# Moving the output weights' sums, the buffers of three pairs and the places of the output splits in a fused retention and feed-forward kernel

## The chip, the cores and the metric

The kernel runs on one core of one Trainium2 chip. The metric is the device time of one execution in microseconds (us): the median of 3 timed runs is 597.18, from 596.79 to 597.63. A separate execution was recorded by the profiler.

## The reference

Three stages follow one another. Stage 1 is a retention layer (batch 2, 8 heads, 768 positions, head size 64) worked in blocks of 64; its output, 1536 tokens by 512, is the input of two feed-forward layers, all in float32:

```
x  = retention(q, k, v, lam)                 # 1536 x 512
h  = x @ w_in;  x1 = relu(h)**2 @ w_out      # 512 -> 2048 -> 512
y  = sigmoid(x1 @ w_gate) * (x1 @ w_val)     # 512 -> 1536
out = y @ w_out2                             # 1536 -> 512
```

## The kernel before, in words

**Precision.** TensorE (PE) multiplies in a rounded float32 format. Each operand is therefore kept as a high part, a rounded copy made by ScalarE (ACT), and a low part, value minus high part, made by VectorE (DVE). Each product takes three matmuls: high by high, high by low, low by high. "Copy" below is the making of a high part, "split" the making of a low part; a tile cannot be used until both are done.

**Tiles.** Tokens lie in three blocks of 512 (TB). The first block goes through a layer directly (`step_1`, `step_2`: `stage_a` multiplies by the input weights, `elem` applies the nonlinearity, `stage_b` multiplies by the output weights); the other two blocks are worked together as a 2 x 2 block product by Strassen's scheme with seven products instead of eight (`strassen`). In the last layer this gives four stretches that the change touches:

- the gate and value stage, 12 steps of 36 matmuls (`step_2`), each with three weight tiles whose low parts `wlo` are made by `split_w` for the next step; in its first half the remaining weights are still converted (`conv_act`, `conv_dve`) and stored in DRAM;
- the pair stage, `strassen` with twelve keys `(2, i, u)`: pairs i = 0 to 5 of hidden tiles, u = 0 for the gate, u = 1 for the value. A key has seven blocks of six matmuls (`block`, L678). ACT takes copies `s` of accumulators (`snap`), DVE adds them (`total`, L692); `use_gate` applies the sigmoid, `use_val` multiplies (L796). Accumulators are added to twice, so a later block of a key waits for the copy or addition that reads the earlier contents;
- the output stage, `blocks_out`: two halves q = 0 and 1 of the output columns, each again with seven products (`PRODUCTS`), each product a sum over the six pairs in groups (`ORDER`); each group is 21 matmuls (42 for the last, with two pairs). For pair i it needs seven matrices, made by sums and differences of the hidden blocks (`raw[0]` to `raw[6]`, made in `use_val` and `later`), as copies and splits in `gq[i]`, and seven combinations of the output weights in `wq[q, i]`;
- the sums of the output weights, `sum_out_w(i)`: a load of two weight tiles (`wr`), four subtractions on DVE (`ws`, L914) and four stores to DRAM; `prepare_w(q, n, i, load, pos)` later loads them into one of two fixed places (`D` and `rows`, taken in turn), copies (L938) and splits (L942) them.

**Seven matrices of a pair.** For pair 0 they go from the raw tiles straight to `gq` (`direct`), with 2.0 us of plan time between pieces. For pairs 4 and 5 `direct` is used too, 0.8 apart, at the places in `DIRECT`. Pairs 1 to 3 (`VIA_DRAM`) are stored as they are made and come back by `through_dram`: three loads of 512 KB and one of 256 KB, with copies (L883) and splits (L886) 1024 or 512 columns wide. Pairs 1 and 2 give up their buffers after q = 0 and are loaded a second time for q = 1.

**Order.** The program is a fixed list. `clock` adds up the time of the matmuls issued (0.2267 us each), and `at(pos, fn)` puts a piece of work on an agenda that is flushed after each block: everything due by the plan's clock is then issued, sorted by place. Every engine takes its instructions in that order and runs ahead as far as its inputs and buffers allow. T4 is the plan's time at which the pair stage starts, T5 that of the output stage, T6 = T5 + 28.56 that of its second half. Loads and most stores are issued by SyncE (SP), also in order.

**Buffers.** `up` has 27 buffers of 2 KB per partition (`unit`), `wp` 27 of 4 KB (`double`), PSUM 8 banks. A tile takes a free buffer when its first instruction is issued, and waits for the readers of the tile that had it before.

Of the kernel before, what the change touches and what calls it, by code (L numbers as in the profile page):

```python
# [38 lines left out]
def retention_moe_kernel(  # L39
# [747 lines left out]
    def pair_in_2(i):  # L787
        gate = {}

        def use_gate(di, t, c, in_psum):  # L790
            r = gate[di, t] = unit("r")
            nc.scalar.activation(r, c, AF.Sigmoid)

        def use_val(di, t, c, in_psum):
            g = unit("g")
            nc.vector.tensor_tensor(out=g, in0=c, in1=gate.pop((di, t)), op=ALU.mult)  # L796
            n = GB.get((di, t))
            raw[n] = g
            if n is not None:
                done(n)  # L800
            if n == 5:
                later()

        raw = {}

        def done(n):
            if i in VIA_DRAM:
                g = raw[n]
                at(clock[0] + 2.5, lambda: nc.sync.dma_start(out=gs_dram[i, :, n], in_=g))

        def total(n, a, b, op):
            raw[n] = unit("gs")
            nc.vector.tensor_tensor(out=raw[n], in0=raw[a], in1=raw[b], op=op)
            done(n)

        def later():


            t = clock[0]
            at(t + 1.5, lambda: total(0, None, 6, ALU.add))  # L820
            at(t + 3.5, lambda: total(1, 0, 4, ALU.subtract))
            at(t + 5.5, lambda: total(2, 4, None, ALU.subtract))
            at(t + 7.5, lambda: total(3, 5, 1, ALU.subtract))
            at(t + 7.5, lambda: direct(i, raw) if i not in VIA_DRAM else raw.clear())

        return [use_gate, use_val]

    GB = {(0, 0): 4, (1, 0): 5, (1, 1): 6}
    VIA_DRAM = (1, 2, 3)
    PIECES = ((0, 1), (2, 3), (4, 5), (6,))  # L830
    gq, wq = {}, {}

# [13 lines left out]
    def block_of(pieces, n):  # L846
        return pieces[n // 2][:, n % 2]

    def direct(i, raw):

        pos = clock[0] if i == 0 else DIRECT[i]
        raw = dict(raw)

        def hi(n):
            if i not in gq:
                new_set(i)
            nc.scalar.copy(block_of(gq[i][0], n), raw[n])

        def lo(n):
            nc.vector.tensor_tensor(  # L860
                out=block_of(gq[i][1], n), in0=raw.pop(n), in1=block_of(gq[i][0], n),
                op=ALU.subtract,
            )

        gap = 2.0 if i == 0 else 0.8
        for k, n in enumerate((4, 5, 1, 0, 2, 3, 6)):
            at(pos + gap * k, lambda n=n: hi(n))
            at(pos + gap * k + 1.2, lambda n=n: lo(n))

    DIRECT = {}  # L870

    def through_dram(i, load, pos):
        raw = {}
# [273 lines left out]
    with tc.manual_schedule():  # L1147
# [97 lines left out]
        for k in range(3 * NF2 - n_out):  # L1245
            convert(T3 + 2.0 + 3.6 * k)
        for i in range(NF2 // 2):
            sum_out_w(i, T4 - 24.0 + 8.0 * i)
        keys = [(2, i, u) for i in range(NF2 // 2) for u in range(2)]
        prepare_a(keys[0], T4)  # L1250
        at(T4 - 28.0, lambda: combine_a((2, 0, 1)))
# [2 lines left out]
        for f in range(NF2):  # L1254
            step_2(f)
        T6 = T5 + 6 * STEP
        through_dram(1, T5 - 13.0, T5 - 6.5)
        through_dram(2, T5 - 4.5, T5 + 0.5)
        through_dram(3, T5 + 1.0, T5 + 6.0)
        DIRECT.update({4: T5 + 11.0, 5: T5 + 16.5})  # L1260
        for n, i in enumerate((0, 1, 2, 3, 4, 5)):
            prepare_w(0, n, i, T5 - 13.5 + STEP * n, T5 - 6.0 + STEP * n)
        for n, i in enumerate((5, 4, 3, 0, 2, 1)):
            prepare_w(1, n, i, T6 - 13.5 + STEP * n, T6 - 6.0 + STEP * n - (2.0 if n == 5 else 0))
        through_dram(2, T6 - 1.0, T6 + 4.8)
        through_dram(1, T6 + 4.0, T6 + 10.0)
        uses = [use for i in range(NF2 // 2) for use in pair_in_2(i)]
        strassen(keys, uses, (None, lambda: close(2)))
        blocks_out()
# [64 lines left out]
```

## Time and profile before

| | before |
|---|---|
| median of 3 timed runs | 597.18 us |
| profiled execution: time | 597.77 us |
| profiled execution: span, first to last instruction | 596.0 us |
| PE busy | 575.7 us (97%) |
| DVE busy | 472.0 us (79%) |
| ACT busy | 366.7 us (62%) |
| granted TensorE clock over the span | 0.999 of full speed |
| pair stage, from its first matmul | 406.34 us |
| output stage, from its first matmul | 533.09 us |

Times in the rows below are microseconds from the span's start. In a row of a timeline the first number is the start, the second the duration from the first to the end of the last of its merged instructions; then the engine, the line of the program, the operation, the tiles (written <- read), the shapes, and "x3" for three instructions. In brackets stands how long the engine was idle before it and whose result ended the wait. Ends of matmuls are modelled, so the distance between starts is the better measure on PE.

### The profile page before, as it was taken

The numbers are of one execution on the slowest core, as the hardware profiler recorded it, in microseconds if no ns is written. First come the engines' busy times: TensorE is split into PE (matmuls) and PEld (weight loads), VectorE is DVE, ScalarE is ACT, GpSimd is POOL, SyncE is SP. The second block draws the span as 40 slices with busy tenths as digits, with TensorE's granted clock in tenths as the row PEclk, the third lists the DMA queues.
The fourth block names the chain that finished last, engine by engine and source line by source line (L and its number), as shares of the span: only waits on it lengthen the run. The fifth ranks groups of instructions, "written<-read, shape, count | busy, mean of one in ns | idle before, by whom it ended". The sixth has DMA issues, their size and how long they took to land.

```text
span 596.0 us, 8997 instructions
## 1 busy us (share of the span) xinstructions
PE 575.7 (97%) x3172; PEld 470.6 (79%) x3172; DVE 472.0 (79%) x726; ACT 366.7 (62%) x599; POOL 47.2 (8%) x48
## 2 busy tenths in 40 slices
PE   8899999989999999999999999999799999989996
PEld 8788888767888888888888888888578888868875
DVE  2689896899788868988777887775789777779964
ACT  4579999996565647666556655534455456377450
POOL 1751100000000000000000000201022210000000
PEclk9999999999999999999999999999999999999999
DMA  8999886772263397999978756857878767445581
GB/s 255 413 405 388 301 291 212 258 286 73 73 210 112 124 328 278 415 410 412 406 244 293 246 174 206 247 175 263 265 183 213 197 196 223 155 158 212 182 321 72
DMA packets 66128, 147.16 MB, mean 247 GB/s; under 512 B 6817, under 2 KB 13985, under 8 KB 66082
## 3 DMA queue, kind: packets, MB, share of 16 engines
q1 hardware_dynamic: 61776, 140.67, 66.7%
q0 software_dynamic: 3360, 3.93, 4.5%
q10 hardware_dynamic: 946, 1.97, 1.0%
q8 instruction: 25, 0.41, 0.3%
q14 instruction: 21, 0.17, 0.1%
HBM read 104.60 MB, written 40.38 MB: 243 GB/s over the span
## 4 chain that ended last, share of the span: by engine, by line
PE 73%; DVE 10%; DMA 8%; ACT 4%; issue 3%; SPq 1%; POOL 0%; DVEq 0%; ACTq 0%
PE p L678 27%; PE p L1056 15%; PE p L472 12%; PE p L985 8%; PE p L486 7%; DMA a<-w 3%; PE p L315 2%; PE p L400 2%; DMA gr<-gs 1%; DMA wt<-wr 1%; DVE xcl L564 1%; DMA decay<-w_dram 1%; DVE at L350 1%; DVE ws L914 1%; PE p L383 1%
## 5 line engine op out<-in xcount | busy, mean ns | idle before, releaser
L678 PE MATMUL p<-xch,ah 128*128 128x512 f32 x280 | 110.4, 394 | 6.9 <-DVE c L692 5.2
L678 PE MATMUL p<-xch,al 128*128 128x512 f32 x280 | 109.1, 390 | 0.0
L678 PE MATMUL p<-xcl,ah 128*128 128x512 f32 x280 | 109.1, 390 | 0.0
L678 PEld LDWEIGHTS p<-xch,ah 128*128 128x128 f32 x280 | 52.6, 188 | 22.2 <-DVE c L692 6.5
L678 PEld LDWEIGHTS p<-xch,al 128*128 128x128 f32 x280 | 52.6, 188 | 11.1
L678 PEld LDWEIGHTS p<-xcl,ah 128*128 128x128 f32 x280 | 52.6, 188 | 10.5
L687 ACT COPY s<-p 128x512 f32<-128x512 f32 x60 | 35.1, 587 | 40.2 <-PE p L678 40.0
L985 PE MATMUL p<-gq,wq 128*128 128x512 f32 x252 | 58.1, 391 | 1.1 <-DVE wq L942 1.1
L985 PEld LDWEIGHTS p<-gq,wq 128*128 128x128 f32 x252 | 47.1, 188 | 11.9 <-DVE wq L942 2.3
L155 ACT ACTIVATE j<-raw 128x512 f32<-128x512 f32 x68 | 45.7, 672 | 13.9 <-issue 5.3
L460 DVE TENSOR_TENSOR wlo<-u,whi 128x512 fp32r<-128x512 f32 x68 | 46.1, 708 | 10.1 <-ACT whi L458 8.1
L692 DVE TENSOR_TENSOR c<-p,s 128x512 f32<-128x512 f32 x60 | 41.1, 686 | 15.5 <-PE p L678 15.1
L181 DVE CUSTOM_DVE_ANT_0 u<-m,r 128x1024 uint16<-128x1024 uint16 x68 | 48.7, 717 | 4.8 <-ACT r L161 1.7
L1056 PE MATMUL p<-g2h,whi 128*128 128x512 f32 x128 | 49.8, 389 | 0.0
L1056 PE MATMUL p<-g2l,whi 128*128 128x512 f32 x128 | 49.8, 389 | 0.0
L1056 PE MATMUL p<-g2h,wlo 128*128 128x512 f32 x128 | 49.8, 389 | 0.0
L472 PE MATMUL p<-xh,wlo 128*128 128x512 f32 x160 | 43.5, 394 | 3.3 <-DVE wlo L460 3.3
L472 PE MATMUL p<-xh,whi 128*128 128x512 f32 x160 | 43.2, 392 | 0.0
L472 PE MATMUL p<-xl,whi 128*128 128x512 f32 x160 | 42.8, 390 | 0.0
L163 ACT ACTIVATE r<-raw 128x512 int32<-128x512 uint32 x52 | 34.6, 666 | 6.9 <-PE p L1056 3.7
L472 PEld LDWEIGHTS p<-xh,wlo 128*128 128x128 f32 x160 | 29.6, 188 | 11.5 <-DVE wlo L460 5.6
L458 ACT CAST whi<-u 128x512 fp32r<-128x512 f32 x68 | 37.9, 615 | 0.5 <-PE p L472 0.5
(127 smaller groups left out, 1043.2 us busy)
## 6 DMA issues: line engine op xcount, KB each, us to landing
raw<-in_w SPq DMA_DIRECT2D x68, 512.0 KB, 6.5
w<-u SPq DMA_DIRECT2D x68, 256.0 KB, 4.6
u<-w SPq DMA_DIRECT2D x52, 256.0 KB, 4.6
a<-w SPq DMA_DIRECT2D x20, 512.0 KB, 4.1
g<-g SPq DMA_DIRECT2D x32, 256.0 KB, 4.4
g<-g SPq DMA_DIRECT2D x16, 512.0 KB, 7.8
gr<-gs SPq DMA_DIRECT2D x15, 512.0 KB, 5.5
kv<-in_kv SPq DMA_DIRECT2D x11, 512.0 KB, 10.1
```

The source lines that it names most:

```text
L155: nc.scalar.activation(j, t[:, :, 1].bitcast(F32), AF.Copy, scale=2.0**-112)
L163: nc.scalar.activation(r, low, AF.Copy, scale=2.0**-29)
L181: nc.vector.tensor_tensor(out=w.bitcast(I32), in0=m, in1=r, op=ALU.add)
L458: nc.scalar.copy(hi, src)
L460: lambda lo=lo, src=src, hi=hi: nc.vector.tensor_tensor(out=lo, in0=src, in1=hi, op=ALU.subtract)
L472: nc.tensor.matmul(acc, lhsT=a[:, kk * P : (kk + 1) * P], rhs=b[:, kk, :], start=i == 0, stop=i == 11,)
L486: nc.tensor.matmul(acc[e], lhsT=a[:, e * P : (e + 1) * P], rhs=b, start=first and i == 0, stop=last and i == 2,)
L678: nc.tensor.matmul(acc, lhsT=w[:, col, kk * P : (kk + 1) * P], rhs=x[:, kk, :], start=start and i == 0, stop=stop and i == 5, skip_group_c ...
L687: nc.scalar.copy(s, acc)
L692: nc.vector.tensor_tensor(out=c, in0=acc, in1=s, op=ALU.add)
L985: nc.tensor.matmul(acc[k], lhsT=a[:, wn], rhs=block_of(b, gn), start=first and n == 0, stop=last and n == 3 * len(group) - 1,)
L1056: nc.tensor.matmul(acc[e, t], lhsT=a[:, e * P : (e + 1) * P], rhs=b[:, t, :], start=first and i == 0, stop=last and i == 2,)
```

## The change

- In the pair stage `later` makes pair 5's four totals 7.5 us of plan time later. Its call at the end now has three cases: pairs in `VIA_DRAM` drop their raw tiles; pair 0 is copied and split by `by_unit` with 4.5 us between pieces; pair 5 by `by_unit` at T5 + 16.5, 0.8 apart.
- `VIA_DRAM` takes in pair 4, so its seven matrices are stored and come back by `through_dram`.
- `by_unit_through_dram` is new: seven loads of 256 KB into 2 KB buffers, 0.7 apart, then `by_unit`. It is used for pair 1 in the first half and for pairs 2 and 1 in the second; before, these used `through_dram` and 4 KB buffers.
- `sum_out_w(i)` is due at T4 - 64 + 9i instead of T4 - 24 + 8i (its load 9 before, its stores 4 after).
- The loads and copies of `prepare_w` stand at places listed one by one instead of at a regular distance.

```diff
@@ -816,17 +816,22 @@
         def later():
 
 
-            t = clock[0]
+            t = clock[0] + (7.5 if i == 5 else 0.0)
             at(t + 1.5, lambda: total(0, None, 6, ALU.add))
             at(t + 3.5, lambda: total(1, 0, 4, ALU.subtract))
             at(t + 5.5, lambda: total(2, 4, None, ALU.subtract))
             at(t + 7.5, lambda: total(3, 5, 1, ALU.subtract))
-            at(t + 7.5, lambda: direct(i, raw) if i not in VIA_DRAM else raw.clear())
+            if i in VIA_DRAM:
+                at(t + 7.5, raw.clear)
+            elif i == 0:
+                at(t + 7.5, lambda: by_unit(i, dict(raw), clock[0], 4.5))
+            else:
+                at(t + 7.5, lambda: by_unit(i, dict(raw), T5 + 16.5, 0.8))
 
         return [use_gate, use_val]
 
     GB = {(0, 0): 4, (1, 0): 5, (1, 1): 6}
-    VIA_DRAM = (1, 2, 3)
+    VIA_DRAM = (1, 2, 3, 4)
     PIECES = ((0, 1), (2, 3), (4, 5), (6,))
     gq, wq = {}, {}
 
@@ -846,10 +851,7 @@
     def block_of(pieces, n):
         return pieces[n // 2][:, n % 2]
 
-    def direct(i, raw):
-
-        pos = clock[0] if i == 0 else DIRECT[i]
-        raw = dict(raw)
+    def by_unit(i, raw, pos, gap):
 
         def hi(n):
             if i not in gq:
@@ -862,12 +864,20 @@
                 op=ALU.subtract,
             )
 
-        gap = 2.0 if i == 0 else 0.8
         for k, n in enumerate((4, 5, 1, 0, 2, 3, 6)):
             at(pos + gap * k, lambda n=n: hi(n))
             at(pos + gap * k + 1.2, lambda n=n: lo(n))
 
-    DIRECT = {}
+    def by_unit_through_dram(i, load, pos):
+        raw = {}
+
+        def bring(n):
+            raw[n] = unit("gr")
+            nc.sync.dma_start(out=raw[n], in_=gs_dram[i, :, n])
+
+        for k, n in enumerate((4, 5, 1, 0, 2, 3, 6)):
+            at(load + 0.7 * k, lambda n=n: bring(n))
+        by_unit(i, raw, pos, 0.8)
 
     def through_dram(i, load, pos):
         raw = {}
@@ -1245,7 +1255,7 @@
         for k in range(3 * NF2 - n_out):
             convert(T3 + 2.0 + 3.6 * k)
         for i in range(NF2 // 2):
-            sum_out_w(i, T4 - 24.0 + 8.0 * i)
+            sum_out_w(i, T4 - 64.0 + 9.0 * i)
         keys = [(2, i, u) for i in range(NF2 // 2) for u in range(2)]
         prepare_a(keys[0], T4)
         at(T4 - 28.0, lambda: combine_a((2, 0, 1)))
@@ -1254,16 +1264,22 @@
         for f in range(NF2):
             step_2(f)
         T6 = T5 + 6 * STEP
-        through_dram(1, T5 - 13.0, T5 - 6.5)
-        through_dram(2, T5 - 4.5, T5 + 0.5)
-        through_dram(3, T5 + 1.0, T5 + 6.0)
-        DIRECT.update({4: T5 + 11.0, 5: T5 + 16.5})
-        for n, i in enumerate((0, 1, 2, 3, 4, 5)):
-            prepare_w(0, n, i, T5 - 13.5 + STEP * n, T5 - 6.0 + STEP * n)
-        for n, i in enumerate((5, 4, 3, 0, 2, 1)):
-            prepare_w(1, n, i, T6 - 13.5 + STEP * n, T6 - 6.0 + STEP * n - (2.0 if n == 5 else 0))
-        through_dram(2, T6 - 1.0, T6 + 4.8)
-        through_dram(1, T6 + 4.0, T6 + 10.0)
+        by_unit_through_dram(1, T5 - 14.0, T5 - 7.0)
+        through_dram(2, T5 - 4.0, T5 + 1.5)
+        through_dram(3, T5 + 1.0, T5 + 6.5)
+        through_dram(4, T5 + 6.0, T5 + 11.5)
+        for n, load, pos in (
+            (0, -21.0, -13.0), (1, -12.0, -1.5), (2, -6.0, 4.0),
+            (3, 1.0, 8.8), (4, 6.0, 13.5), (5, 11.0, 18.3),
+        ):
+            prepare_w(0, n, n, T5 + load, T5 + pos)
+        for n, i, load, pos in (
+            (0, 5, -12.5, -5.0), (1, 4, -7.5, -1.0), (2, 3, -3.0, 3.5),
+            (3, 0, 1.0, 8.0), (4, 2, 6.0, 12.5), (5, 1, 10.0, 15.5),
+        ):
+            prepare_w(1, n, i, T6 + load, T6 + pos)
+        by_unit_through_dram(2, T6 - 7.0, T6 + 5.0)
+        by_unit_through_dram(1, T6, T6 + 10.2)
         uses = [use for i in range(NF2 // 2) for use in pair_in_2(i)]
         strassen(keys, uses, (None, lambda: close(2)))
         blocks_out()
```

## Rows read from the trace of the kernel before

**Rows 1.** Page, part 1: busy time of each engine, share of the span, instructions.

```profile
PE 575.7 (97%) x3172; PEld 470.6 (79%) x3172; DVE 472.0 (79%) x726; ACT 366.7 (62%) x599; POOL 47.2 (8%) x48
```

**Rows 2.** Timeline of PE from the pair stage on: matmuls at its stops.

```profile
418.35 0.39 PE L678 MATMUL p<-xch,al 128*128 128x512 f32 x1
421.39 0.50 PE L678 MATMUL p<-xch,ah 128*128 128x512 f32 x1 [2.65 <-DVE c L692]
...
426.02 0.50 PE L678 MATMUL p<-xch,ah 128*128 128x512 f32 x1 [0.27 <-ACT s L687]
...
432.06 0.50 PE L678 MATMUL p<-xch,ah 128*128 128x512 f32 x1 [0.30 <-DVE c L692]
...
447.11 0.50 PE L678 MATMUL p<-xch,ah 128*128 128x512 f32 x1 [1.11 <-ACT s L687]
...
526.15 0.50 PE L678 MATMUL p<-xch,ah 128*128 128x512 f32 x1 [0.23 <-ACT s L687]
...
531.43 0.50 PE L678 MATMUL p<-xch,ah 128*128 128x512 f32 x1 [2.24 <-DVE c L692]
...
576.83 0.50 PE L985 MATMUL p<-gq,wq 128*128 128x512 f32 x1 [0.45 <-DVE wq L942]
...
583.42 0.50 PE L985 MATMUL p<-gq,wq 128*128 128x512 f32 x1 [0.64 <-DVE wq L942]
```

**Rows 3.** Timeline of PE in the gate and value stage: first reads of `wlo`.

```profile
350.12 1.07 PE L472 MATMUL p<-xh,wlo 128*128 128x512 f32 x4
...
358.28 1.07 PE L472 MATMUL p<-xh,wlo 128*128 128x512 f32 x4
```

**Rows 4.** Chain of waits (start, us, what): the output stage's first piece.

```profile
533.09 36.05 PE p L985 x159
```

**Rows 5.** Timeline of DVE before the stop at 421.39.

```profile
417.44 0.43 DVE L914 TENSOR_TENSOR ws<-wr 128x256 f32<-128x256 f32 x1 [3.91 <-DMA out_t<-o]
...
418.92 0.68 DVE L692 TENSOR_TENSOR c<-p,s 128x512 f32<-128x512 f32 x1
```

**Rows 6.** Timeline of DVE in the gate and value stage: splits of weights.

```profile
348.26 1.90 DVE L460 TENSOR_TENSOR wlo<-u,whi 128x512 fp32r<-128x512 f32 x3 [0.19 <-ACT whi L458]
...
355.83 1.89 DVE L460 TENSOR_TENSOR wlo<-u,whi 128x512 fp32r<-128x512 f32 x3
...
369.39 1.90 DVE L460 TENSOR_TENSOR wlo<-u,whi 128x512 fp32r<-128x512 f32 x3 [1.63 <-ACT whi L458]
...
377.17 1.89 DVE L460 TENSOR_TENSOR wlo<-u,whi 128x512 fp32r<-128x512 f32 x3 [1.63 <-ACT whi L458]
```

**Rows 7.** Timeline of ACT before the stop at 447.11.

```profile
444.00 0.62 ACT L857 CAST gq<-g 128x512 fp32r<-128x512 f32 x1
...
445.95 0.62 ACT L857 CAST gq<-g 128x512 fp32r<-128x512 f32 x1
446.47 0.59 ACT L687 COPY s<-p 128x512 f32<-128x512 f32 x1
```

**Rows 8.** Timeline of ACT before the stop at 526.15.

```profile
524.67 0.94 ACT L938 CAST wq<-D 128x896 fp32r<-128x896 f32 x1
```

**Rows 9.** Timeline of DVE before the stop at 531.43.

```profile
529.55 1.22 DVE L886 TENSOR_TENSOR gq<-gr,gq 128x1024 fp32r<-128x1024 f32 x1
530.69 0.68 DVE L692 TENSOR_TENSOR c<-p,s 128x512 f32<-128x512 f32 x1
```

**Rows 10.** Stretch; busy PE, PEld, DVE, ACT, POOL; clock; DMA share, GB/s.

```profile
524.80:563.30 38.50, 36.03 (x158) 29.17 (x157) 38.21 (x50) 24.21 (x35) 0.00 (x0) 1.00 0.53 174
```

**Rows 11.** Timeline of DVE in the output stage: split of pair 5's weights.

```profile
554.40 1.08 DVE L942 TENSOR_TENSOR wq<-rows,wq 128x896 fp32r<-128x896 f32 x1
```

**Rows 12.** Timeline of SP around T6: output writes, then loads.

```profile
563.30 2.83 SPq L964 DMA_DIRECT2D out_t<-c  x2
...
569.84 1.00 SPq L878 DMA_DIRECT2D gr<-gs  x2
```

**Rows 13.** Line L902, the loads of `sum_out_w`: time from issue to landing.

```profile
DMA to landing us min/median/max: 3.9/4.7/7.1
```

## What is to be expected, worked out before the changed kernel was run

> **What bounds the kernel now.** I read the page's busy times first: TensorE (PE) is busy 97% of the span [rows 1], so only the places where it stands still can give time. The timeline of PE shows them: from the start of the pair stage at 406.34 to the last matmul there are eight stops with a named releaser [rows 2]. A stop costs more than the idle time in its brackets. From 418.35 to 421.39 are 3.04 us against a pace of 0.23 (36 matmuls from 350.12 to 358.28 [rows 3]), so 2.81 for 2.65 idle, and the first matmul after it takes 0.50 instead of 0.39. Idle plus 0.27 is then the price of each: 2.92 at 421.39, 0.54 at 426.02, 0.57 at 432.06, 1.38 at 447.11, 0.50 at 526.15, 2.51 at 531.43, 0.72 at 576.83, 0.91 at 583.42, together 10.05. Each names an addition or a split on DVE or a copy on ACT, engines whose work the trace shows in the order written. So the question for each is what stands in the queue ahead of the instruction that PE wants, and where the change puts that.
>
> T4 below is 406.34, T5 the start of the output stage, 533.09 [rows 4], and T6 its second half, T5 + 28.56 (six groups of 21 matmuls at 0.2267), 561.65.
>
> **Part 1, output weights' sums 40 us earlier.** Before, the sums of pairs 0 to 5 stand at T4 - 24 + 8i, so three of six fall into the pair stage. At 417.44 DVE has stood 3.91 us, since 413.53, at the one whose load is late, and its four subtractions take 1.48 until 418.92 [rows 5]; only then come the two additions that PE wants for the matmul due at 418.58. Their inputs are complete after 36 and 42 matmuls from T4, 414.5 and 415.9. Without the sum DVE makes the one, an `al` split (1.14) and the other from 414.7 on and is done near 417. Gain 2.92. The stop at 432.06 has another such sum of 1.5 us in the queue before it, more than its 0.57: gain 0.57. At 426.02 ACT waits for a split that came late after the stop before; it may go or stay (0 to 0.54), I take 0.25. **Together 3.74**, bounds 0 (the wait passes to the split's own load) and 4.03.
>
> The sums now stand at T4 - 64 + 9i, in the gate and value stage, where nothing stops PE before. There DVE also works off weight conversions, and PE wants the first `wlo` of each step. In step 5 DVE ends it at 348.26 + 0.69 = 348.95 and PE reads it at 350.12: 1.17 to spare. In step 6 it is 355.83 + 0.69 = 356.52 against 358.28: 1.76 to spare [rows 3, 6]. The first sum falls in front of the one (T4 - 64 comes up after the first half of step 4), the second between the two. Sum one, 1.48 less the 0.19 that DVE idles there anyway, makes step 5 late by 0.12. Sums one and two, 2.77 in all, make step 6 late by 1.01. With one restart of 0.27 that is **a new stop of 1.3 us**, both steps together. At steps 8 and 9 DVE stands 1.63 for ACT before its splits [rows 6], which covers sums three to six; without that cover each would cost up to 1.48. Queued behind a sum on DVE are conversions, `wlo` and `gl` splits, and PE waits for the last two; behind its four stores on SP stand the loads of later steps, which SP issues some 5 us ahead of need. Bounds 0 (PE has more room than the trace shows) and 3.0 (both sums pass through whole).
>
> **Part 2, pair 0's splits 4.5 instead of 2.0 apart.** Two of its copies stand on ACT ahead of the `s` copy that ends the stop at 447.11, the ones at 444.00 and 445.95, about 0.52 each from start to next start [rows 7]. At 4.5 apart only the first stays in that product; the next that falls into such a place, the fifth, stands in front of a copy that waits for DVE anyway. **Gain 0.52**, bounds -0.52 (that one costs too) and 1.04. Seven 2 KB buffers stay taken some 15 us longer.
>
> **Part 3, the last product and T5.** Before, ACT has a 1024-wide copy and a weight copy (524.67) ahead of the `s` that PE awaits at 526.15 [rows 8], and DVE has 1024-wide splits and a weight split ahead of the addition at 530.69 that releases PE at 531.43 [rows 9]. Now the first weight split is due at T5 - 11.8, before this product begins, pair 1 comes in 512-wide pieces 0.8 apart, and pair 5's four totals move from T5 + 1.5 to T5 + 9 and later. Small pieces take 0.60 from start to start (three in 1.90 [rows 6]), large ones 1.14 [rows 9]. DVE has two totals, the weight split and an addition at the product's start, 2.8 us from T5 - 11.4 on; then two small pieces while it waits; then, from T5 - 4.2 when ACT has copied the third, that piece, an addition, a multiplication and the fourth piece, 4 x 0.6, so that the wanted addition runs from T5 - 1.8 to T5 - 1.2. PE wants it at T5 - 1.36. Some 0.3 remains of 0.50 + 2.51.
>
> Seven small pieces are 4.2 us, three large and one small 4.0: 0.2 more for a pair. [...]
>
> What was a stop was also time for DVE. From 524.80 to 563.30 it is busy 38.21 of 38.50 us [rows 10]. If T5 comes 2.7 earlier and 1.0 of that work (the weight split, 1.08 long [rows 11]) is moved ahead, DVE is 1.7 later against PE, with 0.2 for the small pieces 1.9. In the output stage the split of pair 5's weights ends at 554.40 + 1.08 = 555.48 [rows 11], and PE reads it first in the third matmul of that group, T5 + 23.8 + 0.45 = 557.35: 1.87 to spare. That is used up, so I put 0.3 for one short stop there. **Gain 3.01 - 0.3 - 0.3 = 2.4**, bounds -0.4 (all returns, and the small pieces cost) and 3.0. Pair 4 through DRAM is seven more stores on SP and four loads instead of none; its splits become three large and one small, 4.0 instead of 4.2. Its loads stand behind a weight load that waits for the weight split two places before, and by my count of SP's queue land about 2 us before DVE comes to them.
>
> **Part 4, the last half.** Before, SP stands 2.83 us at two output writes, and only then issues the loads of pairs 2 and 1, up to 570.84 [rows 12]; they come in a burst, and the weight splits behind them are late at 576.83 and 583.42. Now pair 2's seven loads start at T6 - 7, ahead of those writes, into 2 KB buffers that wait for no matmul; pair 1's start at T6, behind the writes, and need 7 x 0.4 = 3 us of SP. Both are due at T6 + 5 and T6 + 10.2, some 3 us after they land, and DVE has 14 x 0.6 + 4 x 1.0 = 12.4 us of work in the 15 from T6 + 3 to T6 + 18. **Gain 0.72 + 0.91 = 1.63**, bounds -1 (pair 1's loads wait longer behind SP's writes and the last group starts late) and 1.63.
>
> **Sum.** 3.74 + 0.52 + 2.4 + 1.63 - 1.3 = 7.0 us. The profiled execution took 597.77 with a span of 596.0; it would take 590.8. The median of the three timed runs is 597.18, 0.6 below it: 590.2.
>
> **The rivals.**
> (a) DVE is the bound of the output stage. What is to spare there is gone; if one copy or load is late, DVE idles and all that T5 gained is lost again at the groups of pairs 3 to 5. For it: 38.21 of 38.50. Against it: before the last product's pieces DVE has idle time that the earlier weight split and loads now use. Time 590.2 + 2.4 = 592.6.
> (b) The first stops were not the sums' but the 4 KB buffers'. DVE's wait at 417.44 names a DMA, and if the loads of the next products are late for want of buffers, DVE meets them instead. Against it: each sum took two of those buffers, and they are now free. 3.5 us stay: 593.7.
> (c) Slower: the sums wait for their loads in the gate and value stage. Such a load takes 3.9 to 7.1 us to land [rows 13], and SP issues it in order behind conversion loads and stores. If it lands after DVE has come to the sum, DVE stands with the `wlo` splits behind it, as it stood 3.91 at 417.44. Three early sums at that price are 11.7, and step 6 has no slack left: 601.9. It decides once a load is issued later than about 4 us before DVE reaches its sum. Against it: the load's place is 9 us ahead of the sum's.
> (d) The last half gains nothing, because pair 1's loads still stand behind the writes: 591.8.
>
> **How the numbers follow.** The forecast has 0.56 (its own range 588.4 to 591.4), (a) 0.18, (b) 0.08, (c) 0.07, (d) 0.07, and 0.04 is left for gains that cancel. The range goes from 587.6 (every gain at its upper bound, no new stop) to 593.6. A difference of 0.2%, 1.2 us, is about what a measurement of this kernel can tell from none: faster 0.88, no change 0.04, slower 0.08.
>
> **What would show it.** Right: no stop of over 0.7 between T4 + 12 and T4 + 26; a stop of about 1 us in the gate and value stage, released by DVE `wlo`, in the step after the second sum; under 0.6 before T5; none after T6 + 14; DVE without a pause from T5 on. Wrong: long idle time of DVE at the sums, or several stops of PE for `wq` or `gq` between T5 and T6.

## The result and the profile after

The changed kernel took 591.17 us (median of 4 runs, 590.28 to 592.30) where the kernel before took 596.98 (4 runs): ratio 0.9906 [0.9882, 0.9931]. In a second measurement it took 590.58 (590.25 to 590.97) against 597.56: 0.9886 [0.9871, 0.9901]. Forecast were 590.2 and a range of 587.6 to 593.6. The profiled executions took 597.77 and 591.19, 6.58 less.

Page, part 1, of the changed kernel, beside [rows 1]:

```profile
PE 576.1 (98%) x3172; PEld 471.7 (80%) x3172; DVE 474.0 (80%) x732; ACT 366.9 (62%) x605; POOL 47.6 (8%) x48
```

The matmuls are the same 3172 in the same order, so the two traces can be laid on each other by the number of the matmul. The table gives, for stretches named by the times of the kernel before, how much more (+) or less (-) time the changed kernel took from the matmul that begins the stretch to the one that ends it. The forecast of Part 3 is split as it was worked out: 2.7 at the stage's start, 0.3 lost behind it.

| stretch of the kernel before | measured | forecast |
|---|---|---|
| 0 to 340, nothing changed | +0.02 | 0 |
| 340 to 410, gate and value stage: where the sums went | +1.01 | +1.3 |
| 410 to 440, pair stage: where the sums were | -4.14 | -3.74 |
| 440 to 455, pair 0's splits | -0.57 | -0.52 |
| 515 to 533, last product and start of the output stage | -2.23 | -2.7 |
| 533 to 556, output stage, first half | 0.00 | +0.3 |
| 556 to 592, output stage, last half | -0.47 | -1.63 |
| behind the last matmul | -0.23 | 0 |

With 0.02 from 455 to 515 these are the -6.59 by which the span is shorter. Five of the six terms hold within 0.5; one, the last half, is off by 1.16; for the 0.23 behind the last matmul there was no term.

The waits of PE from 340 us on in the changed kernel (engine, line, releaser: us in total, times, longest), where [rows 2] had eight stops:

```profile
PE p L995 <- DVE wq L952: 1.0, 1, 1.0
PE p L678 <- ACT s L687: 0.5, 1, 0.5
PE p L472 <- DVE wlo L460: 0.5, 1, 0.5
PE p L678 <- DVE c L692: 0.4, 1, 0.4
```

Its timeline of PE at these four stops (start us, us, engine, line, operation, tiles, count, and in brackets the idle time before it and the releaser):

```profile
359.15 1.21 PE L472 MATMUL p<-xh,wlo 128*128 128x512 f32 x4 [0.48 <-DVE wlo L460]
...
443.42 0.50 PE L678 MATMUL p<-xch,ah 128*128 128x512 f32 x1 [0.52 <-ACT s L687]
...
525.54 0.50 PE L678 MATMUL p<-xch,ah 128*128 128x512 f32 x1 [0.39 <-DVE c L692]
...
577.06 2.11 PE L995 MATMUL p<-gq,wq 128*128 128x512 f32 x8 [1.00 <-DVE wq L952]
```

The three stops between 421 and 432 are gone, the one at 447 is half as long, the two before the output stage have become one of 0.39, and of the two in the last half one of 1.00 is left. New is the one at 359.15. Its cause and that of the stop at 577.06 stand on DVE's timeline:

```profile
356.94 0.42 DVE L924 TENSOR_TENSOR ws<-wr 128x256 f32<-128x256 f32 x1
...
358.07 0.42 DVE L924 TENSOR_TENSOR ws<-wr,ws 128x256 f32<-128x256 f32 x1
358.41 1.89 DVE L460 TENSOR_TENSOR wlo<-u,whi 128x512 fp32r<-128x512 f32 x3
...
562.84 1.09 DVE L952 TENSOR_TENSOR wq<-D,wq 128x896 fp32r<-128x896 f32 x1 [2.56 <-ACT wq L948]
563.85 2.49 DVE L862 TENSOR_TENSOR gq<-gr,gq 128x512 fp32r<-128x512 f32 x4
567.89 1.09 DVE L952 TENSOR_TENSOR wq<-rows,wq 128x896 fp32r<-128x896 f32 x1 [1.55 <-ACT wq L948]
568.90 3.70 DVE L862 TENSOR_TENSOR gq<-gr,gq 128x512 fp32r<-128x512 f32 x6
...
575.92 1.09 DVE L952 TENSOR_TENSOR wq<-rows,wq 128x896 fp32r<-128x896 f32 x1
```

The second sum runs from 356.94 and the `wlo` splits follow at 358.41. The first of them ends at 359.10; PE read it at 358.28 in the kernel before [rows 3] and, 0.2 behind from step 5, is due at it at 358.51 here. In the last half DVE stands 2.56 and 1.55 us for ACT, and from 567.89 works without a pause until 577.01, when it ends the split that PE waits for. ACT, one step back, stands for the loads of the weights. Behind it come SP's timeline of the same loads and of those before them, SP's waits at that line from 544 to 572 us (us in total, times, longest), and the time from issue to landing of that line from 554 us on:

```profile
561.86 0.94 ACT L948 CAST wq<-D 128x896 fp32r<-128x896 f32 x1 [2.71 <-DMA D<-wt]
...
566.91 0.94 ACT L948 CAST wq<-rows 128x896 fp32r<-128x896 f32 x1 [2.03 <-DMA rows<-wt]
```

```profile
551.22 0.32 SPq L944 DMA_DIRECT2D rows<-wt  x1
551.59 2.80 SPq L876 DMA_DIRECT2D gr<-gs  x6
...
555.67 0.38 SPq L944 DMA_DIRECT2D D<-wt  x1
...
560.86 0.97 SPq L944 DMA_DIRECT2D rows<-wt  x1
```

```profile
SPq L944 <- DVE wq L952: 11.6, 3, 4.7
```

```profile
DMA to landing us min/median/max: 4.0/6.0/6.1
```

The longest of these waits, 4.7 us, is the one before 551.22: that load of weights has a fixed place as its goal, and SP stands until DVE has ended, at 551.19, the split that reads what lies there. Six unit loads of pair 2, written behind it, go out only then. The second half of the stage (T6) starts at 555.73 in this trace, so they start at T6 - 4.1 where the list has them at T6 - 7, and the weight load at 555.67 stands behind them.

Busy time by stretch in the changed kernel (stretch, length; busy PE, PEld, DVE, ACT, POOL; clock; DMA share, GB/s). The first row has the times of [rows 10], but as the stage starts 5.9 us earlier it reaches into the last half; the second is the first half alone:

```profile
524.80:563.30 38.50, 38.12 (x168) 31.10 (x167) 35.57 (x47) 21.89 (x30) 0.00 (x0) 1.00 0.73 267
527.03:555.70 28.67, 28.67 (x127) 23.58 (x126) 28.64 (x36) 18.00 (x24) 0.00 (x0) 1.00 0.63 227
```

```profile
544.00:554.00 10.00, 10.00 (x45) 8.08 (x44) 10.00 (x14) 7.35 (x12) 0.00 (x0) 1.00 0.32 101
554.00:562.00 8.00, 8.00 (x37) 6.64 (x36) 5.97 (x9) 1.08 (x2) 0.00 (x0) 1.00 1.01 361
562.00:570.00 8.00, 8.00 (x37) 6.61 (x36) 5.61 (x8) 5.97 (x11) 0.00 (x0) 1.00 1.02 393
```

In the first half DVE is busy for 28.64 of 28.67 us; what the first row lacks against the 38.21 of [rows 10] is idle time of the last half. From 554 to 570 all DMA engines are busy (share 1.01 and 1.02), and DVE is busy for only 11.58 of 16 us. In the ten microseconds before, the queue is at 0.32. The two weight loads of 448 KB issued at 546.07 and 551.22 took 3.4 us each to land, three of the four issued from 555.67 on 6.0 to 6.1.

### The profile page after: what moved, and what is told of

Read it like the earlier page. It is cut to its first block, busy times and chain, and to the rows that moved or that the text cites. A ratio compares the mean times of both kernels' runs of the same rounds, so it can differ in the third digit from the quotient of the medians.

```text
span 589.4 us, 9045 instructions
## 1 busy us (share of the span) xinstructions
PE 576.1 (98%) x3172; PEld 471.7 (80%) x3172; DVE 474.0 (80%) x732; ACT 366.9 (62%) x605; POOL 47.6 (8%) x48
## 4 chain that ended last, share of the span: by engine, by line
PE 80%; DVE 9%; ACT 4%; DMA 3%; issue 3%; POOL 0%; DVEq 0%; SPq 0%; ACTq 0%
PE p L678 28%; PE p L1066 15%; PE p L472 15%; PE p L486 10%; PE p L995 8%; DMA gr<-gs 2%; PE p L315 2%; PE p L400 2%; DMA decay<-w_dram 1%; DVE at L350 1%; PE p L383 1%; DVE m L189 1%; PE p L411 1%; DVE gq L862 1%; DVE xcl L564 1%
```

## The experiments

All ran beside the kernel before, in three groups of four, each on one chip (before: 598.07, 597.68 and 597.56). The ledger is made as above; all values are against the profiled execution of the kernel before.

| run | 0-340 | 340-410 | 410-440 | 440-455 | 515-533 | 533-556 | 556-592 | median us | ratio |
|---|---|---|---|---|---|---|---|---|---|
| changed | +0.02 | +1.01 | -4.14 | -0.57 | -2.23 | 0.00 | -0.47 | 591.17 | 0.9906 |
| e13, the same again | -0.85 | +0.97 | -4.14 | -0.59 | -2.23 | 0.00 | -0.28 | 590.58 | 0.9886 |
| e1 | -0.80 | +1.00 | -4.14 | -0.05 | +1.23 | +0.31 | -1.23 | 594.03 | 0.9936 |
| e2 | -0.22 | 0.00 | -0.19 | -0.52 | -2.23 | +0.32 | -0.27 | 594.07 | 0.9931 |
| e3 | -0.75 | +0.98 | -4.14 | -0.59 | -2.23 | 0.00 | -0.57 | 590.58 | 0.9878 |
| e4 | -0.64 | +4.19 | -4.14 | -0.59 | -2.23 | 0.00 | -0.86 | 594.32 | 0.9947 |
| e6 | -0.29 | +0.97 | -4.14 | -0.59 | +2.71 | +1.37 | -1.89 | 595.47 | 0.9963 |
| e7 | +1.05 | +0.97 | -4.14 | -0.59 | -1.25 | 0.00 | -1.89 | 591.54 | 0.9899 |
| e8 | -0.49 | +1.00 | -4.14 | -0.55 | -2.24 | 0.00 | -1.47 | 589.27 | 0.9862 |
| e9 | +0.29 | +0.97 | -4.14 | -0.59 | -2.22 | +0.02 | -1.87 | 589.89 | 0.9875 |
| e10 | +0.43 | +0.31 | -4.14 | -0.57 | -2.23 | 0.00 | -1.82 | 589.00 | 0.9861 |
| e11 | -0.78 | +0.31 | -4.14 | -0.57 | -2.23 | 0.00 | -1.82 | 589.43 | 0.9875 |
| e12 | -0.75 | +0.98 | -4.14 | -0.59 | -1.93 | +0.02 | -0.73 | 590.73 | 0.9890 |

The first column is no effect of any edit, since nothing differs there: it is what the program's start varies by from execution to execution (below). A column that repeats to 0.05 is one that the edit didn't touch; the last half differs by 0.19 even between the two executions of the changed kernel.

**e1, the sums alone** (the kernel before, with one line of the change):

```
-            sum_out_w(i, T4 - 24.0 + 8.0 * i)
+            sum_out_w(i, T4 - 64.0 + 9.0 * i)
```

> The kernel before with one edit: the output weights' sums at T4 - 64 + 9i. Theory (places in DVE's queue): the three stops at 421.39, 426.02 and 432.06 go, worth 2.92 + 0.54 + 0.57 = 4.03, one of about 0.75 comes in the gate and value stage after the second sum, and the stops from 447 on stay as they were; 597.2 - 3.3 = 593.9. Rival (4 KB buffers): with the old buffers of pairs 1 and 2 the first stops shrink by less than half, 596 or more. Rival (loads late in the gate and value stage): DVE idle over 2 us at a sum and a time above 597.

594.03, ratio 0.9936 [0.9924, 0.9948], as forecast. Part 1 is worth 4.14 by itself and costs its 1.00 in the gate and value stage by itself. Rival (b)'s price, 3.5 us that stay for the buffers' sake, is refuted: nothing else of the change was there. The stops from 447 to 531 stayed, and behind the last of them the clock fell; of the two in the last half one of 0.35 was left. PE's timeline, and its clock (the figure before the DMA share) behind the stop:

```profile
524.76 0.39 PE L678 MATMUL p<-xch,al 128*128 128x512 f32 x1
527.39 0.79 PE L678 MATMUL p<-xch,ah 128*128 128x512 f32 x1 [2.24 <-DVE c L692]
...
528.40 0.63 PE L678 MATMUL p<-xch,al 128*128 128x512 f32 x1
528.83 0.63 PE L678 MATMUL p<-xch,ah 128*128 128x512 f32 x1
```

```profile
527.30:530.20 2.90, 2.81 (x7) 2.23 (x8) 2.83 (x6) 1.30 (x2) 0.00 (x0) 0.51 0.59 229
```

Matmuls start 0.43 us apart there instead of 0.23, at a clock of 0.51: that is why 515-533 is +1.23 in this run although it is the code of before.

**e2, the sums back** (the changed kernel, without Part 1):

```
-            sum_out_w(i, T4 - 64.0 + 9.0 * i)
+            sum_out_w(i, T4 - 24.0 + 8.0 * i)
```

> The changed kernel with the sums put back to T4 - 24 + 8i. Theory: the stops in the first 26 us of the pair stage come back (3.5 to 4.0) and the one of 0.75 in the gate and value stage goes; 591.2 + 3.2 = 594.4. Rival (the other parts made these sums harmless, by freeing buffers or by spreading pair 0's splits): under 592.

594.07, 0.9931 [0.992, 0.9943]: the time is as forecast, the way to it only in part. The new stop of the gate and value stage goes. Of the pair stage's three stops only the first comes back, with 2.05 us of idle time for 2.65, and behind it the clock stands at 0.52, which costs by estimate some 1.6 of the 3.95 us that come back in 410-440; later than that PE finds the other two copies and additions done. DVE's timeline, PE's, and the clock:

```profile
416.62 0.43 DVE L924 TENSOR_TENSOR ws<-wr 128x256 f32<-128x256 f32 x1 [3.31 <-DMA wt<-wr]
```

```profile
420.57 0.50 PE L678 MATMUL p<-xch,ah 128*128 128x512 f32 x1 [2.05 <-DVE c L692]
```

```profile
420.80:424.00 3.20, 3.20 (x9) 2.49 (x9) 1.47 (x5) 2.78 (x5) 0.88 (x1) 0.52 1.06 404
```

**e3, own buffers for the last half's weights** (the changed kernel; loads at the same places):

```
-            place = (D, rows)[n % 2].rearrange("p a b c -> p (a b) c")
-            t["w"] = place[:, 0:7]
+            if q and n > 1:
+                t["w"] = wp.tile([P, 7, P], F32, tag="w", name="wb")
+            else:
+                place = (D, rows)[n % 2].rearrange("p a b c -> p (a b) c")
+                t["w"] = place[:, 0:7]
```

> The changed kernel with the last four weight combinations of the second half loaded into 4 KB buffers of their own instead of the two fixed places. Theory (the remaining stop of 1.27 near the end comes from ACT standing 2.0 to 2.7 at each weight copy whose load waited for the place): the idle of ACT before the weight copies goes, the stop of 1.27 goes, 591.2 - 1.3 = 589.9. Rival (DVE is simply slower with 14 small pieces): DVE stays busy up to the last weight split, the stop stays above 0.8, 591.0.

Missed. The ratio is 0.9878 [0.9865, 0.9891], but the ledger shows that the last half gave 0.57, no more than in the changed kernel. PE waits 0.9 at the end, and ACT stands for the new buffers as it stood for the old:

```profile
560.92 0.94 ACT L951 CAST wq<-wb 128x896 fp32r<-128x896 f32 x1 [2.59 <-DMA wb<-wt]
```

So the places of these four loads are not what holds them back. The load before them keeps its fixed place: SP still stands 4.7 us at it, until 550.39, with pair 2's loads and these four behind it.

**e4, the sums later, behind the splits** (the changed kernel):

```
-            sum_out_w(i, T4 - 64.0 + 9.0 * i)
+            sum_out_w(i, T4 - 49.0 + 8.163 * i)
```

> The changed kernel with the sums at T4 - 49 + 8.163i, each just behind a step's weight splits and after the last conversion. Theory: the stop of 0.75 (with 0.11 for the restart) in the gate and value stage goes, no stop in the first 26 us of the pair stage comes; 591.2 - 0.9 = 590.3. Rival (DVE has no room left before the pair stage, where the products' own sums are made): a stop of 0.5 to 1.5 appears at T4 or in the first product, 591 to 592.

594.32, 0.9947 [0.9931, 0.9962]: worse by 3.2 in its stretch, and worse than was expected of the rival. The stop at 359.15 went, two others came. PE's timeline, then ACT's:

```profile
400.34 0.96 PE L472 MATMUL p<-xh,whi 128*128 128x512 f32 x3 [2.38 <-ACT whi L458]
...
407.00 1.21 PE L486 MATMUL p<-gh,whi 128*128 128x512 f32 x4 [0.92 <-ACT gh L516]
```

```profile
398.73 1.04 ACT L561 CAST xch<-t 128x1024 fp32r<-128x1024 f32 x1 [3.76 <-DVE t L583]
399.68 1.65 ACT L458 CAST whi<-u 128x512 fp32r<-128x512 f32 x3
```

A sum stands on DVE from 404.14 to 405.69, ahead of the `g` for which the second stop waits. The first came by a detour: DVE works off the combinations of the pair stage's inputs until 398.70, ACT stands 3.76 for the last of them with the weights of the next step queued behind it. Six sums at these places find no room late in this stage; what set it off was not taken apart. The queue is full there (DMA share 0.99 from 380 to 400), but in the changed kernel, which has no stop there, it is as full (1.06 and 1.03).

**e6, the first output weights at their old places** (the changed kernel):

```
-            (0, -21.0, -13.0), (1, -12.0, -1.5), (2, -6.0, 4.0),
+            (0, -13.5, -6.0), (1, -12.0, -1.5), (2, -6.0, 4.0),
```

> The changed kernel with the load and split of the output stage's first weights at their old places (13.5 and 6 us before that stage). Part 3 of the change gained 2.2 to 2.3 us before the output stage: this asks how much of it came from this one move. My theory: the split of 1.08 us comes back on VectorE ahead of c (524.80 in the changed kernel), so the stop of 0.65 there grows by 0.6 to 1.1 to some 1.5: .9906 + .0015 = .992. Rival: the move is free because VectorE has 2.2 us idle at 518 to 520 and only pair 1's 4 KB pieces made the stop: stop unchanged, .9906.

595.47, 0.9963 [0.9949, 0.9976], and no answer to the question. Pair 2's weights use the same place in SBUF and were written between the copy and the split of the first ones: the split waited for pair 2's load (DVE idle 3.55, PE 4.16), and the low part of the first weights came from pair 2's values. It shows two other things: clock 0.50 behind that stop (from 529 to 534), and a last half that gave 1.89 with no edit in it. **e12** asks again, with pair 2's load 2 us later:

```
-            (0, -21.0, -13.0), (1, -12.0, -1.5), (2, -6.0, 4.0),
+            (0, -13.5, -6.0), (1, -12.0, -1.5), (2, -4.0, 4.0),
```

> The changed kernel with the output stage's first weights loaded and split at their old places, and pair 2's weights, which use the same place in SBUF, loaded 2 us later than in the changed kernel, behind that split (in the run with .9963 they were not, so that the low part of the first weights waited 4.2 us for pair 2's load and was taken from its values: that run didn't answer the question). My theory: the 1.08 us of the split come back on VectorE ahead of the c at 524.8: the stop of 0.65 there becomes 1.3 to 1.8, total .9906 + .0015 = .992. Rival (VectorE has 2.2 us idle between 518 and 520, the move is free): stop within 0.2 of 0.65.

0.989 [0.9875, 0.9905]. The split is back on DVE at 520.78, but only 0.30 comes back before the output stage, half of the theory's lower bound, and more than the rival's 0.2. DVE has idle time there that takes most of it: in the changed kernel 0.32 and 0.31 us before the unit splits at 521.26 and 522.26, none here before the one at 521.79, which follows the weight split.

**e7, pair 1 in 4 KB pieces** (the changed kernel):

```
-        by_unit_through_dram(1, T5 - 14.0, T5 - 7.0)
+        through_dram(1, T5 - 14.0, T5 - 7.0)
```

> The changed kernel with pair 1's raw values of the first half in 4 KB pieces again, loads and splits at the new places. Theory 1 (what made the old stop of 2.51 us were 4 KB splits of 1.22 us in a row ahead of c, and their buffers, which come late): the stop before the output stage goes from 0.65 to 1.2 to 2.5; .9916 to .9937. Theory 2 (the old stop came from the first weights' split and from pairs 2 to 4 behind it): within 0.3 of 0.65; .9906.

0.9899 [0.9885, 0.9914]. Theory 1 holds at its lower end: 0.98 comes back before the output stage, with a split of 1.22 ahead of the wanted addition. DVE's timeline, to its last split of weights:

```profile
525.61 1.22 DVE L896 TENSOR_TENSOR gq<-gr,gq 128x1024 fp32r<-128x1024 f32 x1
526.74 0.68 DVE L692 TENSOR_TENSOR c<-p,s 128x512 f32<-128x512 f32 x1
...
576.39 1.09 DVE L952 TENSOR_TENSOR wq<-rows,wq 128x896 fp32r<-128x896 f32 x1
```

But the time is that of the changed kernel, because the last half gave 1.89 instead of 0.47. PE came there 1.94 later than in the changed kernel (1.03 of it from the program's start), DVE's last split only 0.47 later (576.39 against 575.92): the split was no longer late.

**e8, the last half in 4 KB pieces** (the changed kernel, same places):

```
-        by_unit_through_dram(2, T6 - 7.0, T6 + 5.0)
-        by_unit_through_dram(1, T6, T6 + 10.2)
+        through_dram(2, T6 - 7.0, T6 + 5.0)
+        through_dram(1, T6, T6 + 10.2)
```

> The changed kernel with the raw values of the pairs 2 and 1 of the last half in 4 KB pieces again (three of 1024 columns and one of 512), loads and splits at the same new places. VectorE's splits of a pair then take 3 x 1.14 + 0.60 = 4.0 us instead of 7 x 0.60 = 4.2. If the gain of Part 4 (0.56 of 1.63) was held down by the small pieces, the stop of 1.27 shrinks by 0.2 to 0.4 and by more if the seven loads cost more than four: .9896 to .990. If it is held down by the weight loads, the stop stays within 0.2 of 1.27 (.9906 within .0005). If the small buffers are what made the earlier loads possible (my reading of that part), SP waits for 4 KB buffers, later loads and weights go late, and the stop grows by 0.5 to 2: .9915 to .994.

0.9862 [0.9845, 0.9878]: better than expected by any of the three readings. Mine, that the small buffers make the early loads possible, falls: three pieces of pair 2 lay in 4 KB buffers in time to be split from 562.94 on without a pause, where the changed kernel begins at 563.85. DVE:

```profile
562.94 3.49 DVE L896 TENSOR_TENSOR gq<-gr,gq 128x1024 fp32r<-128x1024 f32 x3
567.35 1.09 DVE L952 TENSOR_TENSOR wq<-rows,wq 128x896 fp32r<-128x896 f32 x1 [0.92 <-ACT wq L948]
```

By its second wait DVE has done six of pair 2's seven matrices (in three tiles, 3.49), in the changed kernel four (2.49). The program runs 0.50 ahead of the changed kernel's there, all of it from the start; with that taken off, the wait ends at the same place (567.35 against 567.89), but behind it two matrices less are to be done, so the last split of weights starts 1.04 sooner (574.38 against 575.92).

**e9, own buffers and loads 5 us earlier** (e3, and):

```
-            (0, 5, -12.5, -5.0), (1, 4, -7.5, -1.0), (2, 3, -3.0, 3.5),
-            (3, 0, 1.0, 8.0), (4, 2, 6.0, 12.5), (5, 1, 10.0, 15.5),
+            (0, 5, -12.5, -5.0), (1, 4, -7.5, -1.0), (2, 3, -8.0, 3.5),
+            (3, 0, -4.0, 8.0), (4, 2, 1.0, 12.5), (5, 1, 5.0, 15.5),
```

> The stop of 1.27 us in the last half (DVE wq at 575.92 in the changed kernel) is still without a shown cause: own buffers alone left 1.19 of it. Here the last half's weight loads of the pairs 3, 0, 2 and 1 have own 4 KB buffers and are also written 5 us earlier in SP's list, nothing else. My theory (the loads are issued too late: they land some 2 us after the place of the copy, 6 us after their issue, ScalarE stands at the copy for 2.7 and 2.0 us, VectorE for 2.56 and 1.55): all four land before their copies, both idle times go, VectorE runs its last split some 2 to 4 us earlier, the stop goes; ratio .9885 against the kernel before (.9906 for the changed kernel), 591.2 where before has 598.07. Rival 1 (VectorE's own work, 14 splits of 0.60 and 4 of 1.14 us, is too much for the time that the order gives it): idle time goes but the stop stays above 0.8; .990. Rival 2 (the transfers in that stretch are bound by the queue: a weight load that goes first holds back the unit loads behind it by as much): the wait moves to a unit's copy and a stop of 0.5 to 1.5 us stays, on a unit split or on the same weights; .9895 to .991.

0.9875 [0.986, 0.989], at its forecast of 0.9885 within the interval, and in the way that was forecast. SP's timeline, ACT's, PE's, and two stretches:

```profile
546.64 0.43 SPq L947 DMA_DIRECT2D wb<-wt  x1
```

```profile
559.30 0.94 ACT L951 CAST wq<-wb 128x896 fp32r<-128x896 f32 x1
...
562.23 0.94 ACT L951 CAST wq<-wb 128x896 fp32r<-128x896 f32 x1
```

```profile
569.69 10.59 PE L998 MATMUL p<-gq,wq 128*128 128x512 f32 x46
```

```profile
554.00:562.00 8.00, 8.00 (x37) 6.60 (x37) 7.63 (x11) 3.55 (x6) 0.00 (x0) 1.00 1.03 353
562.00:570.00 8.00, 8.00 (x37) 6.64 (x36) 7.59 (x12) 6.34 (x12) 0.00 (x0) 1.00 1.04 400
```

The queue is as full as before (1.03 and 1.04), but what comes first is what is wanted first. The first of the four loads now goes out ahead of the load at which SP stands, 9 us sooner than in the changed kernel and while the queue is not full (share 0.44 from 544 to 554); the run doesn't tell this from the earlier places of the other three. ACT stands at none of the first three copies and 0.39 at the last, DVE is busy for 15.22 of the 16 us instead of 11.58 and starts its last split at 572.47, and PE runs 46 matmuls through the place of the stop. Rivals 1 and 2 fall; of the wait that rival 2 moves to a unit's copy, ACT shows 1.7 us, which costs PE nothing.

**e13, e10, e11: the changed kernel again, and two versions to beat it.** e10 is e9, e11 is e8, each with the second sum 4 us later, behind the split of step 6:

```
-            sum_out_w(i, T4 - 64.0 + 9.0 * i)
+            sum_out_w(i, T4 - 64.0 + 9.0 * i + (4.0 if i == 1 else 0.0))
```

> The changed kernel itself, unedited, beside the three others on this chip. Its interval (0.9882 to 0.9931) is wider than what the repairs of its last half are worth. Expected .9895 to .991 if its value of .9906 stands; the repaired kernels of the earlier runs (.9875 and .9862) then really are faster than it by 0.2 to 0.4%.

> The kernel with the last half's weights in own buffers and 5 us earlier, and with the second sum of the output weights written 4 us later, so that VectorE does it behind the split of step 6 instead of ahead of it (its load and stores move by the same 4 us). My theory: the stop at 358.3 (0.64 + 0.11 us) goes and nothing else moves: 0.75 us, .9875 - .0013 = .986. Rival (as when all sums were moved: a sum that is late holds something later on VectorE or the transfers): a stop of 0.5 to 2.5 us comes back between 360 and 410; .987 to .990.

> The kernel with 4 KB pieces in the last half, and the second sum written 4 us later. My theory: its last-half stop stays 0.2, the stop at 358 goes: .9862 - .0013 = .985, some 0.5% below the changed kernel. Rival 1 (the same as for the kernel beside it): a stop of 0.5 to 2.5 us between 360 and 410; .986 to .989. Rival 2 (.9862 was luck: the spread of .0016 each way): .987.

The stop at 359 goes in both and no other comes up to 440 (+0.31 instead of +1.01). PE and DVE of e10:

```profile
358.92 1.07 PE L472 MATMUL p<-xh,wlo 128*128 128x512 f32 x4
```

```profile
357.46 1.88 DVE L460 TENSOR_TENSOR wlo<-u,whi 128x512 fp32r<-128x512 f32 x3
359.27 0.41 DVE L924 TENSOR_TENSOR ws<-wr 128x256 f32<-128x256 f32 x1
```

e10 is the fastest kernel: 589.00 (588.33 to 590.15), 0.9861 [0.9844, 0.9878]. On its chip every one of its four runs is below every run of the changed kernel (590.25 to 590.97), by 1.58 in the median; the ledger, without the start, has 2.2 between them. For e11 only the ledger says so: its runs reach from 588.23 to 591.05 and its ratio of 0.9875 [0.9856, 0.9895] is no clear gain on 0.9886. That e8 and e9 beat the changed kernel by themselves is likewise shown by the ledger's last stretch and by the stop, not by the ratios, whose intervals overlap with that of the changed kernel's second measurement.

## Why the prediction was right, and where it was not

**Part 1.** Right in size, and in that the sums stood ahead of the wanted additions. 4.14 was gained, the upper bound (4.03) rather than the 3.74: the stop at 426.02, of which I took 0.25 of 0.54, was a consequence of the one before and went whole. e1 shows it; e2 shows it from the other side with less force, as a part of what comes back there is the clock. One reading was wrong: the sum at 417.44 was not "the one whose load is late". That load, issued at 406.79, had landed at 410.72. The wait ended when the last store of the sum before (`wt<-wr`, issued at 410.93) landed at 417.26, and in e2, where the wait is back, the profile names such a store. By the program only the 4 KB buffer of the new `ws` can wait for it. So it was a wait for a buffer, as rival (b) has it, but moving the sums ended it too.

**The new stop.** Right in place, engine and step; 1.01 instead of 1.3. That both sums together would eat step 6's slack of 1.76 was right: its splits start 2.58 later (358.41 for 355.83) where 2.77 was forecast. PE is then 0.85 late at the first of them, 0.18 of it lost in step 5, and 0.11 more goes at the next matmul; the forecast had 1.01 and a whole restart of 0.27 on top, a part of which lies before that read already. With the second sum behind the split 0.66 of 0.97 went (e9 against e10).

**Part 2.** 0.57 for 0.52; no run takes this part out alone, but without it, in e1, the stretch gives 0.05.

**Part 3.** 2.23 for 2.4, but put together differently: of 3.01 some 0.8 remained before the output stage, not 0.3, and nothing was lost behind it where 0.3 was forecast. That zero was close. The split of pair 5's weights ended at 551.19 and PE read it at 551.29: 0.10 to spare, where the kernel before had 1.70 (557.18 less 555.48; the prediction, which set T5 at 533.09 instead of 532.92, had 1.87). In e2, with nothing to spare at the splits of pairs 4 and 5, 0.32 was lost. Rival (a) is refuted by the 0.00 of 533-556, though DVE was as full as it said. Of the 2.23, pair 1's small pieces are 0.98 (e7) and the earlier first weights 0.30 (e12), each taken out alone; the other 0.95, with pair 4 through DRAM and pair 5's later totals in it, wasn't taken apart. Four small splits take 2.49 (DVE's row at 563.85), 0.60 from start to start as forecast. Six take 3.70 (the row at 568.90), the same columns in three large tiles 3.49 (e8, the row at 562.94): 0.21 more. The 0.4 that the lower bound, -0.4, has for the small pieces is shown by no run.

**Part 4 is the step that failed.** It read: "pair 2's seven loads start at T6 - 7, ahead of those writes", and "DVE has 14 x 0.6 + 4 x 1.0 = 12.4 us of work in the 15 from T6 + 3 to T6 + 18". The loads start at T6 - 4.1, because SP stands 4.7 us at the weight load written before them. The work was right and the time was not: DVE stood still for 4.1 of it, because ACT stood at two weight copies whose loads I had not followed. Those are issued in SP's order among the very unit loads that the change moved forward, into a queue that is full from 554 to 570 (share 1.01 and 1.02), and take 6.0 us; they land 2 to 3 us after ACT has come to them. In the emptier queue just before (share 0.32 from 544 to 554), such a load takes 3.4 us. 0.47 was gained of 1.63. e3 shows that their own places are not the reason, e9, against e3, that earlier issue is, given own buffers: with it the stop goes, 1.87 is gained and the forecast's 1.63 is there. Places without buffers were not tried, since a fixed place is free only after the split two weights before. e8 shows a second way to the same end: with larger pieces ACT and DVE do two more of pair 2's matrices while the second weight load is still on its way, so less is left behind it, though that load lands as late as before. Two of the signs named failed in this half: a stop at T6 + 21, and DVE not without a pause.

A second fault is in the sum. It adds Parts 3 and 4 as if they were independent. In the last half PE waits for work that follows SP, the queue and ACT more than PE, so what PE saves before it waits for there. Three kernels with no repair there point to it: where PE was delayed just before the output stage, the last half gave more, 1.23 in e1 (whose last half is that of before), 1.89 in e6 and in e7, instead of 0.47. The 0.98 that e7 loses before the output stage is paid back at its end in full. A delay further upstream moves SP and ACT along and comes through: e2 and e4 reach the last half 3.1 and 2.8 later than the changed kernel and gave 0.27 and 0.86. This is a reading of five runs made for other questions; none delayed PE alone.

**Rivals (c) and (d).** (c) is refuted: DVE goes into its sums without a pause (356.94 follows on 356.33 + 0.69), so their loads came in time; the same holds for all six sums, whose loads landed at least 1.2 us before them in the changed kernel. (d), nothing gained in the last half, is half true, though for another reason than pair 1's loads behind the writes. (b) was right about the wait and wrong about its price, as e1 shows. That the time itself came out within 1.0 us is luck in part, because the misses cancel: on one side 0.4 too little for Part 1, 0.3 too much for the new stop and the 0.2 behind the last matmul, on the other 1.2 too much for Part 4 and 0.2 for Part 3. That leaves 0.4 between the profiled executions (590.8 forecast, 591.19 measured). The other 0.6 is the step from the profiled execution to the median, which the kernel before had and the changed one did not (591.19 and 591.17). The lower end of the range, 587.6, adds up to 587.5 from the bounds given.

## What to carry to other kernels

When loads are moved forward in one in-order queue, follow the loads that they are moved past: the whole stretch has the same bytes to bring, and what decided here was whether the order of landing was that in which the copying engine asks for them (a stop of 1.00 us in the changed kernel at a DMA share of 1.01 and 1.02, none in e9 at 1.03 and 1.04). A load that waits for its place holds up the loads written behind it: 4.7 us here, with six unit loads. By the reading of five runs above, two gains along one engine's path add up only if what it waits for in the second place follows that engine; otherwise the first is partly paid back at the second (the last half gave 1.89 in e7 instead of 0.47). Two traces of the same program are best laid on each other by the number of the instruction, which separates a term of 0.5 us from a start that varies by 2; a stretch that is compared between them has to be moved along.

## What was not expected of the hardware

After a stop of 2.24 us in e1, 2.05 in e2 and 4.16 in e6 TensorE's granted clock was 0.51 over 2.90 us, 0.52 over 3.20 and 0.50 over 5.00, with matmuls 0.43 apart instead of 0.23. By that difference it cost, as an estimate, some 1.6 (8 matmuls in e1) to 2.5 us (12 in e6) on top of the stop. It does not follow from the length alone: the profiled kernel before has 2.65 us of idle time at 421.39 and the same 2.24 at 531.43 [rows 2] with the clock at 1.00 behind both. Its clock behind the second:

```profile
531.50:534.50 3.00, 3.00 (x13) 2.48 (x14) 2.96 (x5) 1.77 (x2) 0.00 (x0) 1.00 0.55 217
```

What tells the two apart stays open. The two longest stops that the change removed, of 2.65 and 2.24, are no shorter than two of the three with the low clock, and the mean granted clock of the timed runs bears on what that was worth. Of the 26 executions of the kernel before that ran beside the experiments 23 have 0.993 to 0.997 and three 0.999 or 1.000; the eight of the changed kernel all have 0.999 or 1.000. The 23 took 597.87 us in the mean, the three 596.88. An estimate of the clock's part in the gain of the timed runs is therefore 1.0 us, from only three executions on one side. The ledger doesn't have it, as the profiled kernel before is one of the few with the full clock. In e2, which keeps the first long stop, four of five executions have 0.996 or 0.997, in e1, which keeps the last, one of five.

The program's first 340 us, the same in all these kernels, took from 0.85 us less to 1.05 more than in the profiled kernel before, all but 0.15 of it before 60 us; that alone is 0.3% of the time, more than the 1.0 to 1.4 us that the repairs of the last half are worth.
